# Attention, then two feed-forward layers, on one core: the product with v of a head pair made as one unit, its first 64 query columns in a transpose bank and the other 512 in the product bank

## The chip, the core and the metric

The kernel runs on one core of one Trainium2 chip. The metric is the device time of one execution in microseconds (us); lower is better. The engines are TensorE (PE, with its weight loads listed as PEld), VectorE (DVE), ScalarE (ACT), GpSimd (POOL) and SyncE (SP, which issues the DMAs).

## What is computed

Four batches of eight heads of causal attention over 576 positions with 64 values a head, with a bias from the cumulative sum of max(s, 0); then a gated feed-forward layer (512 to 1536 to 512, with an RMS norm before it), then a second one with a GELU (512 to 2048 to 512), on 2304 tokens.

```python
scores = np.where(causal, -1e9, q @ k.T / sqrt(64) + np.minimum(bias, 0.0))
attn = exp(scores - max) / (sum + 1e-09)
x = attn @ v                                   # 4 x 8 heads of 576 x 64 -> x: 2304 x 512
xn = x / sqrt(mean(x * x) + 1e-06) * rms_g
x = (silu(xn @ w_gate) * (xn @ w_val)) @ w_out
out = gelu(x @ w_in) @ w_out2
```

## The kernel before, in words

**A planner writes the order.** The kernel function first lists all its work as operations (`op`, line 311): the engines that may do each one, a function that emits its instructions, a cost in us, an optional due time. Dependencies come from the cells that an operation reads and writes; for a PSUM bank the whole bank is one cell (`cells`, line 240). `plan` (line 1299) then goes through the list: for each engine it takes, among the operations that are ready, the one with the earliest latest-start time (`alap`, lines 1290 to 1297), and on ACT, DVE and POOL it may choose the engine too. Instructions are emitted in that order, and each engine runs its own in order. The due times and costs are constants in `PRM` (line 25): `HD` for the evictions of each head pair's product with v, `FD` for the first layer's early part, `WD` for its weights, `PVC` for the cost of the product with v, and `TA`, the time at which the long chain of the two feed-forward layers is taken to begin (line 1274). The chain's matmuls keep their own order (`chain`, lines 360 to 363).

**Attention, for each of 32 heads** (lines 792 to 813): `scores` (line 535) makes five groups of score matmuls into the banks of kind "s", VectorE adds the mask and takes the minimum of the negated scores, ScalarE takes the exponential; `recip` and `norm` scale; `transp` (line 606) makes four groups of 128x128 transposes in turn into PSUM banks 2 and 3 (kind "t": groups 0 and 2 of a head in bank 2, groups 1 and 3 in bank 3), and ScalarE or VectorE copies each one into a buffer `hd[h, t]`, of which there are 12. After the second head of a pair comes `pv` (line 633), the product with v, in two pieces: piece 0 for queries 0 to 255 (parts of 256 and 128 columns), piece 1 for queries 256 to 575 (parts of 192, 128, 320, 320, 192 and 64). For each part both heads' matmuls run side by side, each on a half of TensorE's columns, so that they are listed as 128*64; each of them is two passes with a weight load each. Each piece has a bank of kind "v" to itself while it runs: bank 4, and for the first eight heads banks 4 and 6 in turn. ScalarE or VectorE copies each piece into `xT`. Then come the sums of squares (`rms_sq`), and after each batch the norm (`rms`, line 669, also through bank 4).

**The first layer's early part** (`fa_tile`, line 714) runs in between: six tiles of 256 tokens through the first two chunks of weights, as 128x256 matmuls into banks 6 and 7. Weights come as 64-bit words and are decoded by ScalarE, VectorE and POOL (`decode`, line 399).

**The chain** (from line 1127) is the rest of the two layers, with matmuls of 384 and 512 columns, in banks 0 to 7. It begins when the attention is done.

Of the kernel before, what the change touches and what calls it, by code (L numbers as in the profile page):

```python
# [15 lines left out]
AF = mybir.ActivationFunctionType  # L16
# [8 lines left out]
PRM = {  # L25
    "G0": 2, "NWS": 18, "NWO": 6,
    "QF": set(range(14)),
    "TIN": [(t * 256, 256) for t in range(6)],
    "PPB": 5, "PTB": 12, "XHB": 7, "HHB": 5,
    "VIRT": 311296,  # L30
    "SLOTS": {
# [14 lines left out]
    "TA": 260.97, "REB": 3, "EARLY": False, "MAG": "AV", "PASS": 0, "ISSUE": 0.6, "INNER": 1.5, "IDLE": 3, "PEN": {}, "PVC": (1.0, 2.25),  # L46
}


# [1 line left out]
def attention_then_swiglu_then_gelu(ctx: ExitStack, tc, qT, kT, vp, s, w1, w2, gT, out):  # L51
    nc = tc.nc
    B, H, D, S = qT.shape
# [10 lines left out]
    TA = sum(n for _, n in TIN)  # L64
# [16 lines left out]
    PB = [pq.tile([P, 512], F32, tag=f"b{i}", name=f"b{i}") for i in range(8)]  # L81
# [7 lines left out]
    def own(name, shape, dt=F32):  # L89
        return const.tile([P] + shape, dt, tag=name, name=name)  # L90

    xT = own("xT", [KT, NT])
# [66 lines left out]
    def get(name, n=None):  # L159
        if n is None:  # L160
            return BUF[name][0]
        return [BUF[f"{name}{i}"][0] for i in range(n)]

    QS, KS, QB, KB, QA, KA, VS, TH = (get(x, 2) for x in ("QS", "KS", "QB", "KB", "QA", "KA", "VS", "TH"))
# [18 lines left out]
    def turn_of(at):  # L183
        return turns[bisect.bisect_right(starts, at) - 1]
# [33 lines left out]
    def size(ap):  # L218
        return 8 if ap.dtype == I64 else 4
# [49 lines left out]
    def isap(x):  # L269
        return hasattr(x, "ap")  # L270
# [37 lines left out]
    def shares(e, name, kw):  # L308
        return e == "G" or e == "V" and not any(isap(x) and "PSUM" in str(x.space) for x in kw.values())

    def op(eng, fn, cost=None, r=None, w=None, due=None, chain=False, dma=False, g=None, after=()):

        o = {"eng": eng, "fn": fn, "due": due, "i": len(ops), "succ": [], "byts": 0, "chain": chain, "g": g}
        costs, ports = [], []
        for e in eng:
            rec = Rec(e)
            if w is None:
                fn(rec)
            costs.append(cost if cost is not None else sum(cost_of(e, *c) for c in rec.calls))
            ports.append(e in "GV" and (w is not None or any(shares(e, *c) for c in rec.calls)))  # L320
        rd, wr = set(), set()
        if w is None:
            for name, kw in rec.calls:
                for k, x in kw.items():
                    if isap(x):
                        (wr if k in OUTS else rd).update(cells(x))
                if dma:
                    n = size(kw["out"])
                    for x in kw["out"].shape:
                        n *= x  # L330
                    inner = all("DRAM" not in str(x.space) or x.tensor.name == virtual.tensor.name
                                for x in (kw["out"], kw["in_"]))
                    o["byts"] += n * (PRM["INNER"] if inner else 1.0)
                    o["inner"] = inner
        else:
            for x in w:
                wr.update(cells(x))
            for x in r or ():
                rd.update(cells(x))
        o["n"] = len(rec.calls) if w is None else 0  # L340
        o["cost"], o["port"] = tuple(costs), tuple(ports)
        deps = set(after)
        for k in rd:
            if k in wrote:
                deps.add(wrote[k])
        for k in wr:
            if k in wrote:
                deps.add(wrote[k])
            deps.update(readers.get(k, ()))
        for at in {k[1] * 64 for k in rd | wr if k[0] == virtual.tensor.name}:  # L350
            _, _, slot, k, _ = turn_of(at)
            users.setdefault((slot, k), set()).add(o["i"])
            if any(c not in wrote for c in wr):
                deps.update(users.get((slot, k - 1), ()))
        for k in rd:
            readers.setdefault(k, set()).add(o["i"])
        for k in wr:
            wrote[k] = o["i"]
            readers[k] = set()
        if chain:  # L360
            if "T" in lastpe:
                deps.add(lastpe["T"])
            lastpe["T"] = o["i"]
        deps.discard(o["i"])
        o["deps"] = sorted(deps)
        for d in o["deps"]:
            ops[d]["succ"].append(o["i"])
        ops.append(o)
        return o
# [67 lines left out]
    hd = {}  # L437
# [6 lines left out]
    def bank(h, kind, i):  # L444
        bs = list(PRM["BANK"][kind]) + (list(PRM["BANKX"].get(kind, ())) if h < PRM["NX"] else [])
        return PB[bs[i % len(bs)]]
# [140 lines left out]
    def norm(h, qb):  # L587
        pt, rc = p_of(h, qb), RC[h % NB]

        def fn(e):  # L590
            if e.tag == "A":
                e.activation(out=pt, in_=pt, func=AF.Copy, scale=rc[:, qb:qb + 1])
            else:
                e.tensor_scalar(out=pt, in0=pt, scalar1=rc[:, qb:qb + 1], scalar2=1.0, op0=ALU.mult, op1=ALU.mult)

        op(PRM["NORM"], fn)
# [9 lines left out]
    def transp(h, t):  # L606
# [11 lines left out]
        def fn(e):  # L618
            if e.tag == "A":
                e.activation(out=pt[:, lo:hi], in_=ps[:, lo:hi], func=AF.Copy, scale=1.0)  # L620
            else:
# [2 lines left out]
        op("AV", fn)  # L624
        hd[h, t] = pt

    PVP = [
# [3 lines left out]
    ]  # L631

    def pv(h, piece, due):

        b_, hh = divmod(h, H)
        q0, n, parts = PVP[piece]
        ps = bank(h, "v", 2 * h + piece)
        t0 = b_ * S + q0
        xo = xT[:, hh // 2, t0:t0 + n]

        def fn(e):
            for i, (t, c, kb, oc, w) in enumerate(parts):
                for j in range(2):
                    r0 = 64 * j
                    e.matmul(ps[r0:r0 + 64, oc:oc + w], VS[h // 2 % 2][:, kb, r0:r0 + 64], hd[h + j, t][:, c:c + w],
                             start=i == 0, stop=i == len(parts) - 1, skip_group_check=True, tile_position=(0, r0))

        op("T", fn, cost=PRM["PVC"][piece])

        def fn(e):  # L650
            if e.tag == "A":
                e.activation(out=xo, in_=ps[:, :n], func=AF.Copy, scale=1.0)
            else:
                e.tensor_copy(out=xo, in_=ps[:, :n])

        op("AV", fn, due=due, g=f"h{h // 2}")

# [128 lines left out]
    def first_weights():  # L786
        for i in range(NW):
            decode(("1", i // 3, i % 3), wa)
            split_w(i, wa, due=PRM["WD"][i], g=f"w{i}")

    setup()
    for h in range(HB):
        prep(h)
        for u in range(5):
            scores(h, u)
        if h == 0:
            first_weights()
        recip(h)
        for qb in range(5):
            norm(h, qb)  # L800
        for t in range(4):
            transp(h, t)
        b_, hh = divmod(h, H)
        if hh % 2:
            for piece in range(2):
                pv(h - 1, piece, PRM["HD"][h // 2])
        if hh % 2:
            rms_sq(b_, hh // 2)
        if hh == H - 1:
            rms(b_)  # L810
            for j, (t0, n) in enumerate(TIN):
                if (t0 + n - 1) // S == b_:
                    fa_tile(j, fill_due)
# [146 lines left out]
    hh = {}  # L960
# [175 lines left out]
    n = 0  # L1136
# [90 lines left out]
    for j, job in enumerate(SJ):  # L1227
# [9 lines left out]
        for x, c in enumerate(cs):  # L1237
            g = nxt
# [35 lines left out]
    T = PRM["TA"]  # L1274
# [118 lines left out]
    for o in ops:  # L1393
        t = max([asap[d] + length(ops[d]) + lat(ops[d]["eng"], o["eng"]) for d in o["deps"]], default=0.0)
        asap[o["i"]] = max(t, ideal.get(o["i"], 0.0))
    start, finish, chosen, stall = plan(asap)
    for _ in range(PRM["PASS"]):
        start, finish, chosen, stall = plan(start)
# [4 lines left out]
    with tc.high_priority(offset=tc.cur_priority - 30000):  # L1403
        for i in sorted(range(N), key=lambda i: (start[i], i)):
# [13 lines left out]
            for ins in traced[k:]:  # L1418
                e = ins.engine
# [52 lines left out]
```

## Time and profile before

| | |
|---|---|
| time, median of 3 runs | 1001.6 us (1001.24 to 1001.68) |
| the profiled execution's own time | 1002.01 us |
| its span, first to last instruction | 1000.2 us |
| TensorE busy | 990.4 us (99%), 5882 matmul instructions |
| weight loads / VectorE / ScalarE / GpSimd busy | 910.7 / 655.0 / 563.0 / 286.1 us |
| DMA | 183.51 MB moved |

Busy times of matmuls overlap where the matmuls do, so a start-to-start distance tells more than a duration. "Idle before" is the engine's idle time ahead of an instruction, with the one that ended it.

### The profile page before, as it was taken

Reading aid. Unit: us, or ns where it says so; the run is one execution under the profiler, and the core shown is the slowest. Engines: PE = TensorE matmul, PEld = TensorE weight load, DVE = VectorE, ACT = ScalarE, POOL = GpSimd, SP = SyncE. Lnnn points to the kernel's source line nnn. Section 1 sums busy time; section 2 is a strip of 40 time slices with the busy share of each in tenths; the row PEclk is TensorE's granted clock in tenths of the full one; section 3 lists DMA queues with packets and bytes.
Section 4 is the critical chain, followed back from the end, with each engine's and each line's share of the span. In section 5 each row is a group of like instructions: output and inputs, shape, how many; then the busy total and the mean of one; then the engine's idle time right before and its main releaser. Section 6 shows DMA issues by size and latency. Waiting matters only on the chain.

```text
span 1000.2 us, 16551 instructions
## 1 busy us (share of the span) xinstructions
PE 990.4 (99%) x5882; PEld 910.7 (91%) x5882; DVE 655.0 (65%) x1532; ACT 563.0 (56%) x1298; POOL 286.1 (29%) x388
## 2 busy tenths in 40 slices
PE   9999999999999999999999999999999999999998
PEld 6777888898999999999999999999889998899987
DVE  8777886777878888546766858874653564353323
ACT  8988786786576555334544436776644463353322
POOL 5666653554332133102322303332320231020000
PEclk9999999999999999999999999999999999999999
DMA  5247766853775762661583676653375045505541
GB/s 181 91 126 183 211 176 177 205 140 118 278 256 225 281 240 98 242 221 43 170 317 144 241 287 231 273 205 123 108 281 221 29 161 232 189 1 197 207 165 63
DMA packets 63050, 183.51 MB, mean 183 GB/s; under 512 B 7028, under 2 KB 23924, under 8 KB 62968
## 3 DMA queue, kind: packets, MB, share of 16 engines
q1 hardware_dynamic: 62968, 182.46, 53.1%
q8 instruction: 46, 0.75, 0.3%
q14 instruction: 36, 0.29, 0.1%
HBM read 122.32 MB, written 44.19 MB: 166 GB/s over the span
## 4 chain that ended last, share of the span: by engine, by line
PE 89%; DVE 4%; ACT 2%; DMA 2%; issue 1%; SPq 1%; POOL 0%; DVEq 0%; ACTq 0%
PE b L208 89%; DVE s L208 1%; ACT s L208 1%; DVE xT L208 1%; SPq L208 1%; DMA s<-in_kT_dram 1%; DMA s<-in_qT_dram 1%; DMA y_d<-sc 0%; DVE b L208 0%; DVE sf L208 0%; POOL wa L208 0%; DVE sc L208 0%; DMA s<-s 0%; ACT st L208 0%; ACT si L208 0%
## 5 line engine op out<-in xcount | busy, mean ns | idle before, releaser
L208 ACT ACTIVATE s<-b 128x384 f32<-128x384 f32 (+1 forms) x267 | 127.6, 489 | 146.4 <-PE b L208 81.2
L208 DVE TENSOR_TENSOR xT<-b,xT 128x384 f32<-128x384 f32 (+1 forms) x158 | 92.6, 599 | 88.7 <-PE b L208 88.0
L208 ACT ACTIVATE b<-b 128x384 f32<-128x384 f32 x125 | 58.2, 478 | 107.8 <-DVE b L208 72.0
L208 POOL TENSOR_TENSOR wa<-wa,st 128x512 int32<-128x512 int32 x50 | 65.9, 1319 | 171.7 <-DVE wa L208 79.0
L208 DVE TENSOR_TENSOR s<-b,s 128x384 fp32r<-128x384 f32 (+1 forms) x121 | 66.4, 553 | 67.3 <-ACT s L208 62.7
L208 PE MATMUL b<-s,w 128*128 128x384 f32 x540 | 107.4, 336 | 0.5 <-DVE s L208 0.3
L208 PE MATMUL b<-s 128*128 128x288 f32 (+11 forms) x420 | 99.2, 361 | 1.8 <-DVE small L208 1.4
L208 PEld LDWEIGHTS b<-s,w 128*128 128x128 f32 x540 | 94.9, 188 | 2.1 <-DVE s L208 1.4
L208 POOL TENSOR_SCALAR wm<-wm 128x512 f32<-128x512 f32 x68 | 41.8, 615 | 140.4 <-ACT wm L208 41.9
L208 PEld LDWEIGHTS b<-s 128*128 128x128 f32 (+1 forms) x420 | 66.9, 192 | 14.8 <-issue 6.3
L208 DVE TENSOR_TENSOR b<-b,s 128x384 f32<-128x384 f32 x82 | 46.1, 562 | 51.6 <-PE b L208 41.4
L208 PE MATMUL b<-sc,w 128*128 128x256 f32 (+1 forms) x396 | 67.3, 304 | 0.0
L208 POOL TENSOR_SCALAR s<-s,small 128x192 f32<-128x192 f32 (+4 forms) x100 | 52.2, 542 | 33.1 <-DVE small L208 11.9
L208 ACT ACTIVATE s<-s,small 128x448 f32<-128x448 f32 (+4 forms) x100 | 55.1, 551 | 9.8 <-DVE small L208 9.6
L208 ACT ACTIVATE st<-st 128x512 int32<-128x512 uint32 x68 | 45.6, 673 | 22.3 <-DMA st<-in_w_dram 22.1
L208 PEld LDWEIGHTS b<-sc,w 128*128 128x128 f32 x396 | 57.1, 189 | 1.0 <-DVE se L208 0.2
L208 PE MATMUL b<-sd,w 128*128 128x384 f32 (+1 forms) x312 | 56.3, 313 | 0.3 <-ACT se L208 0.3
L208 PE MATMUL b<-s,s 128*128 128x384 f32 (+1 forms) x252 | 54.9, 346 | 0.0
L208 PE MATMUL b<-w,s 128*128 128x512 f32 x189 | 51.1, 391 | 0.0
L208 PE MATMUL b<-s,sk 128*128 128x384 f32 x246 | 50.8, 335 | 0.2 <-DVE s L208 0.2
L208 DVE CUSTOM_DVE_ANT_0 s<-b,s 128x288 f32<-128x288 f32 (+4 forms) x100 | 39.3, 424 | 15.7 <-PE b L208 15.5
L208 PEld LDWEIGHTS b<-sd,w 128*128 128x128 f32 x312 | 49.1, 189 | 0.5 <-ACT se L208 0.5
(267 smaller groups left out, 2390.6 us busy)
## 6 DMA issues: line engine op xcount, KB each, us to landing
st<-in_w_dram SPq DMA_DIRECT2D x68, 512.0 KB
s<-s SPq DMA_DIRECT2D x108, 144.0 KB
xT<-y_d SPq DMA_DIRECT2D x3, 1536.0 KB
s<-pc11B SPq DMA_DIRECT2D x6, 768.0 KB
s<-pc21B SPq DMA_DIRECT2D x6, 768.0 KB
out_dram<-xT SPq DMA_DIRECT2D x18, 256.0 KB
s<-in_vp_dram SPq DMA_DIRECT2D x16, 256.0 KB
y_d<-se SPq DMA_DIRECT2D x12, 256.0 KB
```

What stands on the lines that cost most here:

```text
L208: return lambda *args, **kw: f(*[real(x) for x in args], **{k: real(x) for k, x in kw.items()})
```

## The change

The two pieces become one operation. The first 64 query columns of the pair go to columns 0 to 63 of the first transpose bank (bank 2), in matmuls issued first; the other 512 go to a bank of kind "v", which is now chosen by the pair's number. Two evictions follow, of 64 and of 512 columns. The parts of a pair are 64 and then 384, 128, 448, 320, 192 and 64 columns wide. The planner's cost of the unit is 2.95 us, where it was 1.0 and 2.25; its due times and `TA` have new values.

```diff
-    "HD": [48.19, 429.22, 273.85, 177.97, 202.65, 116.26, 599.38, 46.85, 64.88, 418.09, 643.8, 162.22, 92.79, 637.42, 157.16, 161.68],
-    "FD": [(81.45, 266.42), (370.15, 642.27), (623.02, 333.64), (53.78, 479.65), (120.6, 622.93), (183.91, 170.5)],
-    "WD": [123.13, 611.56, 560.46, 472.82, 309.23, 491.67],
-    "TA": 260.97, "REB": 3, "EARLY": False, "MAG": "AV", "PASS": 0, "ISSUE": 0.6, "INNER": 1.5, "IDLE": 3, "PEN": {}, "PVC": (1.0, 2.25),
+    "HD": [320.12, 0.0, 207.58, 451.19, 566.77, 600.81, 477.91, 365.95, 493.19, 193.94, 456.69, 307.96, 565.08, 470.31, 447.99, 142.2],
+    "FD": [(57.92, 59.7), (592.45, 563.4), (134.41, 397.99), (230.51, 353.44), (602.93, 308.94), (425.4, 294.88)],
+    "WD": [464.64, 0.0, 77.62, 632.42, 69.14, 54.99],
+    "TA": 566.79, "REB": 3, "EARLY": False, "MAG": "AV", "PASS": 0, "ISSUE": 0.6, "INNER": 1.5, "IDLE": 3, "PEN": {}, "PVC": 2.95,
...
-    PVP = [
-        (0, 256, [(0, 0, 0, 0, 256), (1, 64, 1, 128, 128)]),
-        (256, 320, [(0, 256, 0, 0, 192), (2, 384, 0, 192, 128), (1, 192, 1, 0, 320), (2, 64, 2, 0, 320),
-                    (3, 64, 3, 128, 192), (3, 256, 4, 256, 64)]),
-    ]
-    def pv(h, piece, due):
+    PVP = [(0, 64, 0, 0, 384), (2, 384, 0, 384, 128), (1, 64, 1, 64, 448), (2, 64, 2, 192, 320), (3, 64, 3, 320, 192),
+           (3, 256, 4, 448, 64)]
+    def pv(h, due):
...
-        ps = bank(h, "v", 2 * h + piece)
+        main, rest = bank(h, "v", h // 2), PB[PRM["BANK"]["t"][0]][:, 0:64]
...
         def fn(e):
+            for j in range(2):
+                r0 = 64 * j
+                e.matmul(rest[r0:r0 + 64, :], VS[h // 2 % 2][:, 0, r0:r0 + 64], hd[h + j, 0][:, 0:64],
+                         start=True, stop=True, skip_group_check=True, tile_position=(0, r0))
...
-        op("T", fn, cost=PRM["PVC"][piece])
+        op("T", fn, cost=PRM["PVC"])
+        for ps, q0, n in ((rest, 0, 64), (main, 64, 512)):
+            xo = xT[:, hh // 2, t0 + q0:t0 + q0 + n]
...
+            op("AV", fn, due=due, g=f"h{h // 2}")
...
-            for piece in range(2):
-                pv(h - 1, piece, PRM["HD"][h // 2])
+            pv(h - 1, PRM["HD"][h // 2])
```

## Rows read from the trace of the kernel before

**Rows 1.** The page: span; busy time of each engine, its share and instructions.
```profile
span 1000.2 us, 16551 instructions
PE 990.4 (99%) x5882; PEld 910.7 (91%) x5882; DVE 655.0 (65%) x1532; ACT 563.0 (56%) x1298; POOL 286.1 (29%) x388
```

**Rows 2.** Busy time of each engine in three stretches: PE, PEld, DVE, ACT, POOL; clock, DMA.
```profile
50.00:100.00 50.00, 48.47 (x367) 36.90 (x366) 38.60 (x142) 41.17 (x118) 32.73 (x55) 1.00 0.57 154
...
250.00:300.00 50.00, 48.77 (x277) 47.18 (x276) 39.51 (x69) 31.81 (x60) 17.75 (x18) 1.00 0.74 267
...
400.00:450.00 50.00, 50.00 (x291) 50.00 (x290) 24.09 (x46) 17.78 (x38) 2.52 (x3) 1.00 0.62 232
```

**Rows 3.** Waits of TensorE over the span: us in total, times, longest.
```profile
PE b L208 <- DVE small L208: 1.4, 1, 1.4
PE b L208 <- DVE s L208: 1.1, 3, 0.6
...
PE b L208 <- ACT xT L208: 0.6, 1, 0.6
```

**Rows 4.** Timeline of TensorE around one pair's piece 0: start, us, instruction.
```profile
107.09 0.43 PE L208 MATMUL b<-sb,s 128*64 128x256 f32 x1
...
107.36 0.38 PE L208 MATMUL b<-sb,s 128*64 128x256 f32 x1
...
107.57 0.27 PE L208 MATMUL b<-sb,s 128*64 128x128 f32 x1
...
107.68 0.27 PE L208 MATMUL b<-sb,s 128*64 128x128 f32 x1
...
107.89 0.82 PE L208 MATMUL b<-s 128*128 128x288 f32 x4
```

**Rows 5.** The same timeline around that pair's piece 1.
```profile
109.82 0.51 PE L208 MATMUL b<-sc,w 128*128 128x256 f32 x3
110.26 0.38 PE L208 MATMUL b<-sb,s 128*64 128x192 f32 x1
...
110.48 0.33 PE L208 MATMUL b<-sb,s 128*64 128x192 f32 x1
...
110.64 0.27 PE L208 MATMUL b<-sb,s 128*64 128x128 f32 x1
...
112.26 0.22 PE L208 MATMUL b<-sb,s 128*64 128x64 f32 x1
...
112.32 0.22 PE L208 MATMUL b<-sb,s 128*64 128x64 f32 x1
...
112.47 1.69 PE L208 MATMUL b<-sc,w 128*128 128x256 f32 x12
```

**Rows 6.** The same timeline, 256-column matmuls with no 128*64 work behind them.
```profile
118.94 0.52 PE L208 MATMUL b<-sc,w 128*128 128x256 f32 x3
119.30 0.72 PE L208 MATMUL b<-s 128*128 128x320 f32 x4
```

**Rows 7.** Evictions by shape on ACT and DVE: count, busy us, mean ns, idle before.
```profile
L208 ACT ACTIVATE xT<-b 128x512 f32<-128x512 f32 x18 | 10.8, 598 | 17.0 <-PE b L208 16.9
L208 ACT ACTIVATE xT<-b 128x320 f32<-128x320 f32 x14 | 6.1, 434 | 10.9 <-PE b L208 10.8
...
L208 DVE CUSTOM_DVE_ANT_0 s<-b,s 128x64 f32<-128x64 f32 x20 | 4.4, 219 | 0.0
```

**Rows 8.** Timeline of all engines: a piece 1 that waited for piece 0's eviction.
```profile
186.97 0.27 PE L208 MATMUL b<-sf,s 128*64 128x128 f32 x1
...
188.95 0.36 ACT L208 ACTIVATE xT<-b 128x256 f32<-128x256 f32 x1
...
189.37 0.38 PE L208 MATMUL b<-sf,s 128*64 128x192 f32 x1 [0.56 <-ACT xT L208]
```

**Rows 9.** The timeline of TensorE again: a piece 1 with transposes right behind it.
```profile
103.22 0.22 PE L208 MATMUL b<-sg,s 128*64 128x64 f32 x1
...
103.38 0.99 PE L208 MATMUL b<-ident,sk 128*128 128x128 f32 x7
```

More of the change, by code (lines that the diff above doesn't have):

```diff
@@ L625, in transp, with fn @@
         hd[h, t] = pt
-    PVP = [
[3 rows of a table removed]
-    ]
-    def pv(h, piece, due):
+    PVP = [(0, 64, 0, 0, 384), (2, 384, 0, 384, 128), (1, 64, 1, 64, 448), (2, 64, 2, 192, 320), (3, 64, 3, 320, 192),
+           (3, 256, 4, 448, 64)]
+    def pv(h, due):
         b_, hh = divmod(h, H)
-        q0, n, parts = PVP[piece]
-        ps = bank(h, "v", 2 * h + piece)
-        t0 = b_ * S + q0
-        xo = xT[:, hh // 2, t0:t0 + n]
+        main, rest = bank(h, "v", h // 2), PB[PRM["BANK"]["t"][0]][:, 0:64]
+        t0 = b_ * S
         def fn(e):
-            for i, (t, c, kb, oc, w) in enumerate(parts):
+            for j in range(2):
+                r0 = 64 * j
+                e.matmul(rest[r0:r0 + 64, :], VS[h // 2 % 2][:, 0, r0:r0 + 64], hd[h + j, 0][:, 0:64],
+                         start=True, stop=True, skip_group_check=True, tile_position=(0, r0))
+            for i, (t, c, kb, oc, w) in enumerate(PVP):
                 for j in range(2):
                     r0 = 64 * j
-                    e.matmul(ps[r0:r0 + 64, oc:oc + w], VS[h // 2 % 2][:, kb, r0:r0 + 64], hd[h + j, t][:, c:c + w],
-                             start=i == 0, stop=i == len(parts) - 1, skip_group_check=True, tile_position=(0, r0))
-        op("T", fn, cost=PRM["PVC"][piece])
[L650 to L656, printed above, removed]
+                    e.matmul(main[r0:r0 + 64, oc:oc + w], VS[h // 2 % 2][:, kb, r0:r0 + 64], hd[h + j, t][:, c:c + w],
+                             start=i == 0, stop=i == len(PVP) - 1, skip_group_check=True, tile_position=(0, r0))
+        op("T", fn, cost=PRM["PVC"])
+        for ps, q0, n in ((rest, 0, 64), (main, 64, 512)):
+            xo = xT[:, hh // 2, t0 + q0:t0 + q0 + n]
+            def fn(e, ps=ps, xo=xo):
+                if e.tag == "A":
+                    e.activation(out=xo, in_=ps, func=AF.Copy, scale=1.0)
+                else:
+                    e.tensor_copy(out=xo, in_=ps)
+            op("AV", fn, due=due, g=f"h{h // 2}")
     RO = [0, 128, 256, 384, 448]
```

## The prediction

> **What bounds the kernel now.** I read the page's busy times first: TensorE is busy for 990.4 of 1000.2 us, and no other engine passes 66%, weight loads aside [rows 1]. That share hides small gaps, because overlapping matmuls count as busy, so the next view is the table by stretch: in the chain (400 to 450 us) TensorE is full, and in the attention (50 to 100 us) and at the change to the chain (250 to 300 us) it lacks 1.5 and 1.2 us of 50, with the clock granted in full [rows 2]. VectorE and ScalarE still have about 9 us of 50 free in the attention stretch. Third, the waits: TensorE waits for others nine times, 5.5 us in all. The longest, 1.4 us, lies at the very start, and one of 0.6 us is for ScalarE's write of `xT`, which is the eviction of a piece of the product with v [rows 3]. So the time is TensorE's own stream. An edit is worth what it takes out of that stream, plus what it changes in about 5 us of waits. Last, I read start-to-start distances in the timeline around two pieces [rows 4, 5]; they show what a piece costs besides its columns.
>
> **The change part by part.**
>
> *Columns.* A pass of 256 columns takes 0.21 us (107.36 to 107.57), one of 192 takes 0.16, of 128 0.11, of 64 0.06 [rows 4, 5]: in proportion, with no floor down to 64. Before, a pair has parts of 256, 128, 192, 128, 320, 320, 192 and 64 columns, 1600 in all; after, 64, 384, 128, 448, 320, 192 and 64, again 1600. This costs nothing either way. One part fewer over 16 pairs, two heads and two passes is 64 fewer instructions (5882 to 5818), whose fixed share these rows put at a few ns each.
>
> On weight loads the Trainium skill ("TensorE: Matmul & The Clock Gate", Part 3) says that a load overlaps a running matmul only when the row group differs, and here all share one; it puts a load at columns divided by 1.2, which is 53 ns for 64 columns. By that each pass would show its load, and the two passes a pair saved would bring an estimated 1.7 us over 16 pairs on top of my sum. The 128-column pass at half the time of the 256-column one [rows 4] leaves no room for a fixed 53 ns, so I take zero.
>
> *Entering and leaving the half-width form.* Three 256-column matmuls take 0.36 us up to the next full-width work (118.94 to 119.30) [rows 6], but 0.44 up to a piece (109.82 to 110.26) [rows 5]: 0.08 us at entry. The first pass of a piece is longer than its twin: 0.27 against 0.21 for 256 columns [rows 4], 0.22 against 0.16 for 192 [rows 5]: 0.06. The last pass is followed after 0.21 where 128 columns need 0.11 [rows 4], and after 0.15 where 64 need 0.06 [rows 5]: about 0.10 at exit. Together 0.24 us a piece. There are 32 pieces before and 16 units after, so 16 x 0.24 = **3.8 us** go. All of it lies in TensorE's stream, beside nothing. What no row shows is a move from one bank to another within half-width work, from the 64 columns to the main bank. Its ends are nothing (both halves stay in that form; inside a piece the parts follow without a gap) and a whole 0.24 us, which would take all of the 3.8 back. I take nothing, since it is the form that changes at the gaps in the rows.
>
> *Evictions.* Before, 320 columns at 0.43 us and 256 at about 0.36 [rows 7, 8]; after, 512 at 0.60 and 64 at about 0.22 (the nearest row is a VectorE read of 64 columns from PSUM) [rows 7]. That is 0.79 against 0.82 on engines with room [rows 2]: nothing. Only the last pair of each batch has the norm behind it, with an eviction 0.16 us longer; four times, 0.6 us at most if no other matmul is ready, none if one is. I take none and keep 0.6 for the range.
>
> *The bank of the products.* After the first eight heads both pieces use bank 4, so the second may not start until the first is evicted. Once this stopped TensorE: ScalarE was busy elsewhere, took the eviction up at 188.95, 2.0 us after the piece's last matmul began, and the piece 1 behind it waited 0.56 us [rows 8]. With one unit a pair there is nothing to wait for: **0.6 us** go. Everything TensorE issues waits behind it in order, so the wait was paid in full.
>
> *The transpose bank.* The new wait: the next pair's transposes of groups 0 and 2 may write bank 2 only after the 64 columns are evicted. They are issued first, so 2.7 us of the unit's own columns (1600 less 64, two passes at 0.00083 us a column, from 0.21 over 256) run meanwhile. Uncovered, the nearest price is the 0.56 us above, a wait of TensorE on the same kind of eviction. Ends: 0 and 16 x 0.56 = 9.0 us. I take 0: behind 12 of 16 pieces 1 TensorE goes on with scores or first-layer matmuls, and only behind 4 with transposes [rows 9].
>
> *The new due times and `TA`.* They move which ready operation goes first, not how many there are; DMAs and SP's issues are the same in number. TensorE's columns are the same in any order, so only the waits can differ. They are 5.5 us now; less the start and the one that goes, 3.5 us could vanish, and I bound the loss by as much again as the gain, about 4 to 6 us. Where only the order is in question I take no change.
>
> *Sum.* 3.8 + 0.6 = 4.4 us. The profiled execution took 1002.0 us in all (span 1000.2 [rows 1] and 1.8 around it), which gives 997.6; it lies 0.4 above the median of the runs, 1001.6, so the forecast there is **997.2 us**. The measurement can tell about 0.2%, 2.0 us, from no change.
>
> **The rivals.**
>
> *A. The gaps go and the waits go too.* If the new order also removes most of the remaining waits: 997.2 - 3.5 = 993.7. For it: nothing in the chain has to stop TensorE [rows 2]. Against: several waits end on masks and norms that this change leaves alone [rows 3].
>
> *B. The new order waits as much as the change saves.* Each of a dozen handovers a little later, in other places than now, at 0.3 to 0.6 us each [rows 3], costs 3 to 5 us: 1000.2 to 1002.2. For it: due times, `TA` and the unit of TensorE's work all move at once, and one uninterrupted unit of nearly 3 us leaves scores behind it waiting, whose exponentials ScalarE then gets late. Against: TensorE stops only nine times now, so there is mostly something ready.
>
> *C. The transpose bank becomes the wait.* ScalarE or VectorE takes up the 64 columns only in its own order, behind other work, as at 188.95 [rows 8], and TensorE has nothing but the next transposes. In all 16 pairs: 997.2 + 9.0 = 1006.2, slower. It cancels the gain from 8 pairs on, and is slower by over 0.2% from 12 on. Against: the 2.7 us of cover, and 12 of 16 pieces followed by other work. On why the columns don't help, the Trainium skill ("PSUM — Partial Sum Buffer", "PSUM bank collisions raise a hardware error") says that two engines must not touch one bank and quadrant at once even at different columns; no run here shows such an overlap, and the kernel's own bookkeeping keeps whole banks apart.
>
> *D. The unit does not stay in one form.* If changing the bank inside the unit costs a gap like the one saved, only the 0.6 us is left: 1001.0.
>
> **How the numbers follow.** Forecast (997.2, its own range 995.5 to 999.0) 0.50; A 0.14; B 0.20; C 0.11; D 0.05. Faster by over 0.2% (below 999.6) are the forecast and A: 0.64. Within 0.2% are D, and of B most: 0.22. Slower (above 1003.6) are C and the far end of B: 0.14. The range 993.7 to 1003.5 leaves out C and a part of A.
>
> **What would show it.** Right: 16 half-width runs instead of 32, each of about 2.85 us with 64-column parts at both ends, 5818 matmul instructions, a start-to-start distance from the 64 columns to the 384 with no gap, no wait of the product with v on ScalarE's write of `xT`, and waits of about 5 us in all. Wrong: waits of TensorE on `xT` ahead of transposes (C), more waits on exponentials, copies of transposes or loads between 20 and 290 us (B), or a gap of 0.1 us or more inside the unit (D).

## The result, and the profile after

The changed kernel takes 1008.15 us (median of 7 runs, 1004.17 to 1008.89) against 1001.6 for the kernel before (seven runs too, 1000.55 to 1004.32): a ratio of 1.0055, 95% interval 1.0037 to 1.0072. It is **slower**, by 5.5 us on the ratio. The forecast was 997.2 us, with a range up to 1003.5.

The page of the changed kernel, span and busy times, and its granted clock in 40 slices:

```profile
span 1006.9 us, 16422 instructions
...
PE 992.5 (99%) x5818; PEld 907.3 (90%) x5818; DVE 649.5 (65%) x1510; ACT 569.7 (57%) x1311; POOL 292.4 (29%) x397
...
PEclk9998999999899999999999999999999999999999
```

The 64 matmul instructions fewer are there, 5818 against 5882 [rows 1], and TensorE is still busy for 99%. New are two slices in which the clock was not granted in full. The table by stretch shows them beside the stretch that answers to [rows 2]:

```profile
50.00:100.00 50.00, 48.51 (x333) 35.72 (x332) 36.32 (x129) 40.33 (x111) 30.75 (x48) 0.93 0.44 125
...
250.00:300.00 50.00, 45.68 (x250) 43.83 (x249) 41.41 (x85) 31.26 (x56) 17.20 (x17) 0.93 0.67 239
...
400.00:450.00 50.00, 50.00 (x291) 50.00 (x290) 26.86 (x53) 18.61 (x38) 3.83 (x4) 1.00 0.60 221
```

The clock column fell from 1.00 to 0.93 twice, and TensorE lacks 4.3 us of 50 at the change to the chain, where it lacked 1.2. In the chain nothing differs. Narrower stretches of the changed kernel show what went ahead of the first fall, and the second one:

```profile
72.00:75.00 3.00, 1.93 (x10) 1.03 (x8) 2.97 (x11) 3.00 (x10) 1.90 (x5) 1.00 0.52 161
75.00:82.00 7.00, 6.78 (x22) 4.09 (x24) 5.10 (x21) 4.82 (x16) 5.59 (x10) 0.51 0.16 52
82.00:85.00 3.00, 3.00 (x27) 1.96 (x24) 0.26 (x1) 2.06 (x7) 0.61 (x1) 1.00 0.00 0
...
262.80:269.70 6.90, 5.21 (x15) 4.81 (x16) 6.90 (x11) 3.78 (x5) 1.40 (x1) 0.51 0.77 315
```

At the first fall TensorE was busy for 1.93 of 3 us, then worked 7 us at half of its clock (1.2 GHz instead of 2.4), then in full again. The Trainium skill ("TensorE: Matmul & The Clock Gate", Part 1) has this as its rule: the clock goes to half when TensorE has had little to do. The trace agrees here: the clock was 0.51 behind 1.93 of 3 us of work. Not every such gap was followed by a fall; the last section has the others.

The unit itself, in the timeline of TensorE (start, us, instruction):

```profile
105.10 0.27 PE L208 MATMUL b<-sf,s 128*64 128x64 f32 x1
...
105.21 0.22 PE L208 MATMUL b<-sf,s 128*64 128x64 f32 x1
...
105.27 0.49 PE L208 MATMUL b<-sf,s 128*64 128x384 f32 x1
...
107.80 0.22 PE L208 MATMUL b<-sg,s 128*64 128x64 f32 x1
...
107.96 0.62 PE L208 MATMUL b<-sd,w 128*128 128x256 f32 x3
```

It runs from 105.10 to 107.96, 2.86 us, where the two pieces took 0.80 and 2.21 [rows 4, 5]: 0.15 us less and one entry of 0.08 us less for each pair, 3.7 us over 16 pairs. Fifteen of the 16 units take 2.85 to 2.87 us; the other, at 80.57, runs partly at half clock. The move from the 64 columns to the main bank (105.21 to 105.27) has no gap. This part of the forecast (3.8 us) came true.

The waits of TensorE were twelve, 5.5 us in all, in a list of nine rows of which [rows 3] shows three (the middle number of a row is how often). Now they are fifteen, and these are the four largest of ten rows:

```profile
PE b L208 <- ACT sg L208: 2.9, 2, 2.7
PE b L208 <- DVE s L208: 1.7, 2, 1.5
PE b L208 <- DVE xT L208: 1.6, 2, 1.2
PE b L208 <- POOL s L208: 1.5, 3, 0.5
```

All of the list comes to 10.3 us. The 0.6 us on ScalarE's write of `xT` is gone, as forecast, but 4.8 us of others came. The two on `xT` here are not evictions of the product: they are the norm, whose second half waits in the same bank until VectorE has scaled `xT` with the first.

The largest wait lies at the end of the attention. First the kernel before, the timeline of TensorE from the first matmul of the last batch's norm:

```profile
241.05 1.18 PE L208 MATMUL b<-small,s 128*128 128x2 f32 x10
242.09 3.12 PE L208 MATMUL b<-sc,w 128*128 128x256 f32 x24
245.04 0.88 PE L208 MATMUL b<-sd,w 128*128 128x256 f32 x6
...
247.85 0.87 PE L208 MATMUL b<-sd,w 128*128 128x256 f32 x6
...
249.46 1.70 PE L208 MATMUL b<-sd,w 128*128 128x256 f32 x12 [0.32 <-ACT se L208]
...
263.48 0.63 PE L208 MATMUL b<-w 128*128 128x512 f32 x2
```

Then the changed kernel, the same view from the same point:

```profile
249.41 1.59 PE L208 MATMUL b<-sd,w 128*128 128x256 f32 x12
250.83 1.18 PE L208 MATMUL b<-small,s 128*128 128x2 f32 x10
...
260.52 0.72 PE L208 MATMUL b<-ident,small 64*128 64x64 f32 x3 [0.43 <-DVE xT L208]
263.93 0.69 PE L208 MATMUL b<-sg,w 128*128 128x384 f32 x1 [2.69 <-ACT sg L208]
265.17 3.89 PE L208 MATMUL b<-sg,w 128*128 128x384 f32 x11 [0.55 <-DVE sg L208]
...
271.36 0.63 PE L208 MATMUL b<-w 128*128 128x512 f32 x2
```

Before, 48 first-layer matmuls of 256 columns (24, 6, 6 and 12) still stood behind the norm's first one and ran while VectorE and ScalarE worked through the norm and the splitting of its results for the chain. After, none is left: all had run before 250.83. TensorE takes the first chain matmuls that need nothing of the last batch, and then waits 2.69 us, and the clock falls during that wait (0.51 from 262.80 to 269.70). The two-matmul step of the chain at 263.48 and 271.36 is a mark that both kernels pass: 7.9 us later, though all units but one were shorter. From the mark to the end it is 736.7 us before and 735.5 after. So the whole loss arose before the chain.

### The profile page after: what moved, and what is told of

The parts are those of the page before. It is cut to its first block, busy times and chain, and to the rows that moved or that the text cites. A ratio compares the mean times of both kernels' runs of the same rounds, so it can differ in the third digit from the quotient of the medians.

```text
span 1006.9 us, 16422 instructions
## 1 busy us (share of the span) xinstructions
PE 992.5 (99%) x5818; PEld 907.3 (90%) x5818; DVE 649.5 (65%) x1510; ACT 569.7 (57%) x1311; POOL 292.4 (29%) x397
## 5 line engine op out<-in xcount | busy, mean ns | idle before, releaser
L208 POOL TENSOR_SCALAR s<-s,small 128x192 f32<-128x192 f32 (+3 forms) x100 | 52.9, 549 | 30.2 <-DVE small L208 14.5
L208 ACT ACTIVATE s<-s,small 128x192 f32<-128x192 f32 (+4 forms) x100 | 55.0, 552 | 6.4 <-DVE small L208 6.0
L208 DVE CUSTOM_DVE_ANT_0 s<-b,s 128x448 f32<-128x448 f32 (+4 forms) x100 | 39.5, 426 | 13.3 <-PE b L208 12.7
```

The costliest lines, as they stand in the source:

```text
L208: return lambda *args, **kw: f(*[real(x) for x in args], **{k: real(x) for k, x in kw.items()})
```

## The experiments

The theory behind them: the unit takes some 3.9 us out of the stream, and the order that the planner makes around it with the new due times costs more, in waits and in two falls of the clock. The main rival: the unit itself, by holding the transpose bank, stretches the attention in any order. A second rival: the falls cost nothing.

### The unit with the due times of before

```diff
-    "HD": [320.12, 0.0, 207.58, 451.19, 566.77, 600.81, 477.91, 365.95, 493.19, 193.94, 456.69, 307.96, 565.08, 470.31, 447.99, 142.2],
+    "HD": [48.19, 429.22, 273.85, 177.97, 202.65, 116.26, 599.38, 46.85, 64.88, 418.09, 643.8, 162.22, 92.79, 637.42, 157.16, 161.68],
...
-    "TA": 566.79, ...
+    "TA": 260.97, ...
```

`FD` and `WD` are those of before as well; `PVC` stays 2.95.

> The unit of the change with the due times and TA of before (cost 2.95). Theory: the unit takes about 3.9 us out of TensorE's stream, and the loss of the change comes from the order that the planner makes around it: 10.3 us of waits against 5.5, two of them long enough (1.2 and 2.7 us, at the norms of the first and the last batch) that the granted clock falls to half for 6.8 us after each, 3.4 us lost per fall. If the new due times alone are to blame, this run has waits as before and takes about 997 to 998 us; if the unit needs due times of its own, whatever they were, a long wait at the last norm is still there and it takes 1002 to 1009 us. Rival (the unit itself: the 64 columns hold the transpose bank and stretch the attention in any order): slower than before, 1003 us or more, with waits of TensorE on evictions of xT or transposes spread over the attention.

Measured: 1007.21 us (4 runs; ratio to before 1.005, 1.0035 to 1.0065), granted clock 0.995 and waits of 10.5 us in the profiled run. The end of the attention, timeline of TensorE:

```profile
247.10 1.59 PE L208 MATMUL b<-sd,w 128*128 128x256 f32 x12
248.53 1.17 PE L208 MATMUL b<-small,s 128*128 128x2 f32 x10
...
262.41 0.69 PE L208 MATMUL b<-sg,w 128*128 128x384 f32 x1 [2.60 <-ACT sg L208]
```

The new due times are not to blame by themselves. With the old ones, too, the unit leaves no first-layer matmul behind the last norm, and the same wait is there. This run alone would also fit the rival; the next pair tells them apart.

### The unit and the pieces, each in an order of its own

The due times and `TA` were found by a search of the same kind for the unit and for the pieces: from the kernel's own values or from random ones, whichever gave the better list, and then step by step, with the kernel's own planner, for an early end of TensorE's list. How far each search went is not known, so the two orders may not be equally good.

For the unit:

```diff
+    "HD": [641.77, 628.23, 558.42, 387.8, 570.46, 314.85, 322.29, 139.22, 633.63, 530.95, 300.22, 555.49, 597.24, 272.63, 309.69, 192.23],
+    "FD": [(400.85, 564.42), (408.83, 248.7), (412.67, 532.45), (241.85, 451.86), (325.3, 633.33), (388.0, 395.09)],
+    "WD": [597.82, 157.66, 212.0, 290.57, 569.02, 152.38],
+    "TA": 364.79, ...
```

For the pieces:

```diff
+    "HD": [164.72, 53.92, 280.03, 646.26, 65.58, 264.1, 162.51, 339.69, 246.01, 110.68, 205.95, 248.78, 144.87, 626.72, 238.34, 161.68],
+    "FD": [(610.01, 192.18), (262.61, 190.84), (375.74, 578.83), (196.63, 315.02), (613.47, 363.35), (183.91, 170.5)],
+    "WD": [602.92, 94.86, 579.55, 600.98, 175.99, 207.92],
+    "TA": 433.93, ...
```

> The unit of the change with a third set of due times and TA, in whose list the last batch's norm is covered by other work. Theory (the unit is worth 3.9 us, and the order decides the rest): waits of about 5 us, clock 1.0, 996 to 999 us. Rival (the unit stretches the attention in any order): waits of 8 us or more, a long one at the end of the attention, 1002 us or more.

> The two pieces of before, also with due times and TA found anew in the same manner. It tells what a better order alone is worth. Theory: 998 to 1002 us, and the unit in its new order is 2 to 5 us faster than this. Rival (the unit stretches the attention): this one is at least as fast as the unit in its new order.

Measured: the unit takes 995.34 us (5 runs, 994.33 to 995.89; ratio 0.9939, 0.9927 to 0.9952), the pieces 999.65 (11 runs; ratio 0.9984, 0.9975 to 0.9992). The unit, 0.7 us under its band, is 4.3 us faster than the pieces, and 0.6% (6.1 us on the ratio) faster than the kernel before. The first row of its list of waits:

```profile
PE b L208 <- DVE small L208: 1.8, 3, 1.4
```

The list comes to 4.9 us, that of the pieces to 4.0, and the clock is granted in full in both. The last norm of the unit's run, timeline of TensorE:

```profile
234.58 1.18 PE L208 MATMUL b<-small,s 128*128 128x2 f32 x10
235.62 3.12 PE L208 MATMUL b<-sc,w 128*128 128x256 f32 x24
238.57 0.88 PE L208 MATMUL b<-sd,w 128*128 128x256 f32 x6
...
242.99 1.70 PE L208 MATMUL b<-sd,w 128*128 128x256 f32 x12 [0.32 <-ACT se L208]
...
257.11 0.63 PE L208 MATMUL b<-w 128*128 128x512 f32 x2
```

The 48 matmuls are there again, the norm begins 6.5 us earlier than in the kernel before, and the mark comes at 257.11. So there is an order in which the unit does not stretch the attention: the main rival, which had it do so in every order, falls. This version beats both kernels.

### Work in the waits, to hold the clock

Extra matmuls of 512 columns in the changed kernel's order, which nothing reads, ahead of the first norm's second half and of the chain's matmul that waited 2.69 us.

```diff
+    FILL = [(413, 614, 3, 'mask'), (1904, 1905, 6, 'xT')]
+    for i0, other, n, src in FILL:
+        pb = next(b for b in PB if (b.tensor.name, 0) in ops[other]["wr"])
+        mv = mask[:, 0:512] if src == "mask" else xT[:, 0, 768:1280]
...
+            for _ in range(n):
+                e.matmul(pb, ident, mv, start=True, stop=True)
+            f(e)
```

Operations 413 and 1904 are the two that waited; the extra matmuls write the bank of a later operation (614 and 1905), which is free by then. The second run (e5) has 1 and 3 for 3 and 6.

> The changed kernel in its own order, with nine extra 512-column matmuls that nothing reads: three (0.43 us each) ahead of the second half of the first batch's norm, six ahead of the chain's matmul that waited 2.7 us. They do not shorten any wait on another engine, they only keep TensorE at work in it. Theory (the two falls of the clock come from those waits and cost 3.4 us each): granted clock 1.0 throughout, and 6 to 7 us less than the changed kernel: 1001 to 1002.5 us. Rival (the clock falls for another reason, or the falls are not what costs the time): the clock still falls, 1008 us or, with the extra matmuls' 3.9 us on top, up to 1012 us.

Measured: 1007.53 us (5 runs), clock 1.000 in the profiled run and 0.998 to 0.999 in the others. The clock stayed up and the time did not come back: neither the theory's number nor the rival's falling clock. The timeline shows why:

```profile
259.64 5.42 PE L208 MATMUL b<-xT,ident 128*128 128x512 f32 x12
```

Six matmuls are twelve passes here, of some 0.4 us each (the next matmul starts at 264.50); I had priced the six at one pass each. Counting the three at the first norm too, they held TensorE 3.5 us longer than the waits had lasted, which is most of what the falls of the clock cost (below). So the number was halved:

> As e2_fill_waits, with one extra matmul instead of three and three instead of six: in e2 each of them took two passes of 0.43 us, twice what its text assumed, so that they held TensorE 1.4 and 2.1 us longer than the waits they were to fill. Theory (each fall of the clock costs about 3 us, as the stretches of e2 where it stayed up suggest): granted clock 1.0 throughout and 1001 to 1003 us. Rival (the falls cost nothing, because the stage is bound by ScalarE and VectorE there): 1007 to 1008 us as in e2.

Measured: 1004.27 us (8 runs, 1003.98 to 1004.8; ratio to before 1.0027, 1.0016 to 1.0037), clock 1.000, 3.9 us less than the changed kernel and 1.3 above the expected band. The stretches of the first fall and the end of the attention in this run:

```profile
75.00:82.00 7.00, 6.99 (x49) 4.69 (x50) 4.95 (x20) 6.73 (x20) 6.30 (x11) 1.00 0.17 49
```

```profile
257.89 2.84 PE L208 MATMUL b<-xT,ident 128*128 128x512 f32 x6
260.65 0.44 PE L208 MATMUL b<-sg,w 128*128 128x384 f32 x1
...
265.99 0.63 PE L208 MATMUL b<-w 128*128 128x512 f32 x2
```

In the 7 us from 75 on TensorE started 49 matmuls where the changed kernel started 22, and the mark comes at 265.99 instead of 271.36: 5.4 us earlier in the same order, with four useless matmuls on TensorE. These fitted into the waits: from the last norm's 64x64 matmuls to the chain's waiting one it is 3.41 us with them (257.24 to 260.65) as without (260.52 to 263.93), and at the first norm 2.65 and 2.64. Of the 5.4, 1.5 are lost in the chain (737.0 us from the mark to the end), where the list has a wait of 1.0 us for a load of the first layer's pieces that the changed kernel does not have (0.8 in e2); its cause stays open. The second rival falls: the two falls cost about 5.4 us together.

The seven runs of the changed kernel agree. Their mean clocks are 0.993 to 0.997 and their spans 1007.1 to 1002.4 us, but span times clock, which takes out what the clock withheld, is 999.3 to 1000.1 in every one, to the half us that three decimals of the clock allow. The span before is 1000.2. So I estimate that without a fall the changed kernel would be about as fast as the one before: the new waits eat what the unit saves, and the clock makes the loss.

### One due time alone

```diff
-    "FD": [(57.92, 59.7), (592.45, 563.4), (134.41, 397.99), (230.51, 353.44), (602.93, 308.94), (425.4, 294.88)],
+    "FD": [(57.92, 59.7), (592.45, 563.4), (134.41, 397.99), (230.51, 353.44), (602.93, 308.94), (600.0, 620.0)],
```

> The changed kernel with one pair of due times changed: the last of the six first-layer tiles is due at 600 to 620 instead of 425.4 to 294.88, so that the planner gives TensorE the attention first and has first-layer matmuls left when the last norm begins. Theory (the loss at the end of the attention comes from first-layer matmuls that were used up before the last norm: none left after it in the changed kernel, 48 left before): matmuls of 256 columns behind the last norm's first, no wait over 2.2 us and no fall of the clock at 255 to 270 us, the fall at 75 us still there: 1002 to 1006 us. Rival (the unit's hold on the transpose bank delays the last norm whatever the tile's due time): 1007 us or more.

Measured: 1009.8 us (6 runs, 1006.31 to 1012.11; ratio 1.0078, 1.0061 to 1.0094): a miss, in the band of the rival. The profiled run took 1007.76, with a clock of 0.998; the others had 0.994 to 0.998. Its last norm:

```profile
247.49 1.18 PE L208 MATMUL b<-small,s 128*128 128x2 f32 x10
...
250.73 0.87 PE L208 MATMUL b<-sd,w 128*128 128x256 f32 x6
252.34 1.69 PE L208 MATMUL b<-sd,w 128*128 128x256 f32 x12 [0.74 <-ACT se L208]
...
263.85 0.44 PE L208 MATMUL b<-sg,w 128*128 128x384 f32 x1 [0.22 <-ACT sg L208]
...
269.27 0.63 PE L208 MATMUL b<-w 128*128 128x512 f32 x2
```

As the theory said, eighteen first-layer matmuls are held back, the wait ahead of the chain is 0.22 us, no wait passes 2.2 us and the clock does not fall there. Against it, the fall at 75 us did not come in this run, and one came at 235 us, behind waits of 1.69 and 0.85 us on POOL's normalised scores. All waits come to 13.0 us, 3.5 of them on these scores. I take it that the held-back matmuls had filled gaps in the attention and are missing there; no run shows that apart. The last norm begins at 247.49, 3.3 us earlier than in the changed kernel and 6.4 later than before. The rival's reason is not borne out: no wait is on an eviction of the product, and e3 has the norm early with the same unit. But covering the last norm does not by itself bring the time back.

### Another order for the same unit

A fourth set of due times, from a less successful search:

```diff
+    "HD": [160.03, 12.53, 333.51, 475.59, 626.04, 157.92, 29.12, 45.09, 220.32, 278.91, 380.13, 314.97, 343.72, 22.0, 640.48, 108.56],
+    "FD": [(142.61, 65.44), (334.41, 63.9), (96.13, 278.4), (137.77, 504.42), (371.35, 400.23), (430.83, 563.53)],
+    "WD": [101.84, 2.54, 241.7, 606.57, 378.61, 48.58],
+    "TA": 362.88, ...
```

> The unit with a fourth set of due times and TA, found like those of e3_unit_new_order but with a poorer list. It tells how far the order alone moves the time with the unit unchanged. Theory (order decides): between e3_unit_new_order and the change, 997 to 1003 us, with waits between theirs. Rival (the unit has one price in any order): within 1 us of e3_unit_new_order.

Measured: 1000.53 us (10 runs; ratio 0.9994, 0.9985 to 1.0003), waits 8.0 us and clock 1.000 in the profiled run. Between the two, as expected. With nothing but due times changed, the same unit takes from 995.3 to 1009.8 us.

### The price of a half-width run by itself

With a change of form (e8), in `pv` between the 64 columns and the rest:

```diff
+            e.matmul(main[:, 0:2], ident, ident[:, 0:2], start=True, stop=True)
```

Without one (e9):

```diff
+            for r0 in (0, 64):
+                e.matmul(main[r0:r0 + 64, 0:2], ident[:, 0:64], ident[:, 0:2],
+                         start=True, stop=True, skip_group_check=True, tile_position=(0, r0))
```

> The unit in the order of e3_unit_new_order, with one two-column full-width matmul (two passes) between the 64 columns and the other 512 of each unit, its result overwritten: the unit is again two half-width runs. Theory (a second half-width run costs 0.24 us in entry, first pass and exit, beside its columns): 3.8 us more than e9_split_half, in which the same two columns are done at half width; about 999 to 1002 us, and in the trace 32 half-width runs. Rival (the changes of form cost nothing by themselves, the two pieces were slow for their banks or their number): within 1 us of e9_split_half.

> As e8_split_full, but the two extra columns are done at half width by two matmuls side by side, so that the unit stays one half-width run: the control. Theory: the extra passes cost 0.05 to 0.1 us each, two a unit, so 1 to 3 us over the 995.3 us of e3_unit_new_order: 996 to 998.5 us. Rival: as e8_split_full within 1 us.

Measured: 1002.93 us (11 runs, 1001.71 to 1004.44) and 998.94 (5 runs, 996.83 to 999.27), 4.0 us apart where 3.8 was expected; the profiled clocks are 1.000 in both. The medians lie 0.9 and 0.4 over their bands. The trace of e8 has 32 half-width runs, as expected. The timelines of TensorE inside one unit, first the full-width columns between (e8):

```profile
116.45 0.22 PE L208 MATMUL b<-sb,s 128*64 128x64 f32 x1
...
116.61 0.38 PE L208 MATMUL b<-ident 128*128 128x2 f32 x2
116.92 0.54 PE L208 MATMUL b<-sb,s 128*64 128x384 f32 x1
```

then the control (e9):

```profile
114.71 0.22 PE L208 MATMUL b<-sb,s 128*64 128x64 f32 x1
...
114.77 0.23 PE L208 MATMUL b<-ident 128*64 128x2 f32 x4
114.86 0.52 PE L208 MATMUL b<-sb,s 128*64 128x384 f32 x1
```

From the last pass of the 64 columns to the 384 it is 0.47 us with a change of form and 0.15 without. Not all of the difference is the form's. A whole unit takes 2.86 us in e3 and 3.32 in e8 (116.34 to 119.66). Two full-width passes of two columns cost an estimated 0.21 us of that, after the norm's ten that take 1.04 (234.58 to 235.62 in e3), which leaves 0.25 for the second entry, first pass and exit: the forecast's 0.24. That the medians lie 4.0 us apart, so near to 3.8, is partly luck, as the full-width columns are in it, and the waits of e8 are 1.2 us shorter than those of e9 (4.0 and 5.2).

A pair in e4 settles the banks and the number of pieces. There the planner once put both pieces of a pair right behind each other, in two banks, and they take 56.11 to 58.97, 2.86 us, like a unit. So it is the change of form that costs time, whatever the number of banks.

## Why the prediction was wrong

The profiled spans of the runs without extra matmuls in one table. The last column is the span less the waits of TensorE and less what the clock withheld, which is one minus the mean granted clock, times the span:

| run | span, us | waits, us | clock | rest, us |
|---|---|---|---|---|
| before | 1000.2 | 5.5 | 1.000 | 994.7 |
| pieces, new order (e4) | 997.9 | 4.0 | 1.000 | 993.9 |
| the change | 1006.9 | 10.3 | 0.993 | 989.6 |
| unit, old due times (e1) | 1005.7 | 10.5 | 0.995 | 990.2 |
| unit, one tile late (e6) | 1005.9 | 13.0 | 0.998 | 990.9 |
| unit, other order (e7) | 998.5 | 8.0 | 1.000 | 990.5 |
| unit, new order (e3) | 993.4 | 4.9 | 1.000 | 988.5 |

The rest is 994 to 995 us with the pieces and 988 to 991 with the unit, in every order tried. That is the change's own work, and it gained 3 to 6 us, 4.4 between the means. What remains, the waits and the clock, goes with the order.

- **Columns, entering and leaving:** right, 3.7 us for 3.8, and found again as 0.25 us a unit in e8. The cover that the prediction gives the 64 columns, 2.7 us, is about 2.5 by its own factors; nothing hung on it. The rule on weight loads of the Trainium skill ("TensorE: Matmul & The Clock Gate", Part 3), which the forecast weighed, would have made each pass show its load; the pass of 64 columns in the unit takes 0.06 us (105.21 to 105.27), so the row decided rightly.
- **The bank of the products:** right; the wait of 0.6 us went.
- **Evictions and the transpose bank:** right. No wait on an eviction of the product stands in the list after, so rival C did not occur, and nor did rival D.
- **The new due times and `TA`:** the step that failed. It said that in any order "only the waits can differ", and "Where only the order is in question I take no change", and bounded the loss by 4 to 6 us. The waits grew by 4.8 us, inside that bound, and the likeliest value should not have been zero. By e1 it is not the new values as such: the old ones lose as much around the unit. It is the order that the planner makes of the unit with either set. What no term held is the clock: two of the waits were followed by 7 us each at half clock, 5.4 us by e5 and 7.0 by the table, which also counts half clock in which TensorE stood idle (it was busy for 5.21 of the 6.90 us of the second fall). With them the sum is -3.7 + 4.8 + 5.4 = 6.5, against 6.7 between the two spans.
- **The count of the waits:** the prediction reads nine stops of TensorE, here and against rival B, but nine are the rows of the list; the stops are twelve. Their sum, 5.5 us, is right.
- **Rival B** named the right mechanism, an order that waits as much as the change saves, at 1000.2 to 1002.2 with a chance of 0.20, and without the falls of the clock, by the estimate under e5, it would have been about right. It missed the clock, and it looked in the wrong place, at late exponentials; the longest wait was at the end of the attention, behind the last norm, with its cover used up.

The trace of before held the hint: the waits were few because 48 matmuls stood behind the last norm, which no dependency keeps there (in the changed kernel they ran earlier), only the planner's choice. I listed the waits that were there, not the work that hid those that were not.

The pieces with the due times of the change were not run, so the share of these values in the loss is known only through e1, where the old values lose about as much.

## What to carry to other kernels

When an edit goes with a new plan, price both: the work removed is read from rows and held in all five orders here, but what work still stands behind each long dependent step (here a norm, 9.7 us from 250.83 to 260.52 in the changed kernel) bears on whether it reaches the end, and in e6 cover alone did not bring it back. Before a forecast of "same waits", name for each such step what covers it and what keeps that cover in its place. Give a wait on TensorE a second price for the clock that may fall after it, as a chance and not as a certainty, and judge a new building block only with an order found for it, against the old one with an order found as carefully.

## What was not expected of the hardware

In the changed kernel, waits of 1.19 us (TensorE busy for 1.93 of the 3 us around it) and of 2.69 us were each followed by about 7 us at 0.51 of the clock. The length of a wait does not settle it. In e1 a wait of 1.61 us (to 107.03) was followed by a clock of 1.00, and one of 0.55 (to 250.61) by some 3 us at 0.50 (252 to 255). In e6 the same matmul at 75 us waited 1.20 us, and the clock stayed:

```profile
72.00:75.00 3.00, 1.71 (x9) 1.05 (x8) 2.97 (x9) 2.96 (x9) 1.92 (x5) 1.00 0.60 184
75.00:82.00 7.00, 7.00 (x50) 4.64 (x51) 4.93 (x21) 6.73 (x20) 6.30 (x10) 1.00 0.16 46
```

What decides between them stays open, and it differs between runs of one program: the seven of the changed kernel have mean clocks of 0.993 to 0.997. Fp32 matmuls of 512 columns that nothing needs, of 0.8 to 0.9 us each, held the clock in e5 (1.000 in all eight runs).
